# Rounds of two token tiles in the stage between two attention loops

## The chip, the cores and the metric

The kernel runs on one core of one Trainium2 chip. The metric is the device time of one execution in microseconds (us). A core has a matrix engine (PE, whose weight loads the profile shows apart as PEld), three engines for elementwise work (VectorE: DVE; ScalarE: ACT; GpSimd: POOL) and a queue that issues transfers (SyncE: SP). Each engine works through its own instructions in a fixed order and waits on semaphores. Matrix products land in PSUM, in banks; everything else is in SBUF or in HBM.

## The reference

Four residual blocks on 2048 tokens of width 576: grouped attention with one key and value head (A), linear attention with learned feature maps (B), A again, B again, with the same weights in both rounds.

```python
def _A_ref(x, wq, wk, wv, wo):          # 32 query heads of 18, one key and one value head
    q = heads(x @ wq); k = x @ wk; v = x @ wv
    p = _softmax(einsum("bhqd,bkd->bhqk", q, k) * Dh ** -0.5)
    return merge(einsum("bhqk,bkd->bhqd", p, v)) @ wo

def _B_ref(x, wqkv, w_phi, wo):
    q, k, v = split_heads(x @ wqkv)
    pq = einsum("bhsd,hdf->bhsf", q, w_phi); pk = einsum("bhsd,hdf->bhsf", k, w_phi)
    phi_q = concat([_softmax(pq), _softmax(-pq)]); phi_k = concat([_softmax(pk), _softmax(-pk)])
    kv = einsum("bhsf,bhsd->bhfd", phi_k, v); z = einsum("bhsf->bhf", phi_k)
    return merge(einsum("bhqf,bhfd->bhqd", phi_q, kv) / (einsum("bhqf,bhf->bhq", phi_q, z) + 1e-6)) @ wo

x = x + _A_ref(_layernorm(x), A_wq, A_wk, A_wv, A_wo)
x = x + _B_ref(_layernorm(x), B_wqkv, B_w_phi, B_wo)
x = x + _A_ref(_layernorm(x), A_wq, A_wk, A_wv, A_wo)
x = x + _B_ref(_layernorm(x), B_wqkv, B_w_phi, B_wo)
```

## The kernel before

The 2048 tokens are 16 token tiles of 128 (tile 0 to tile 15), and two tiles are a pair. The program has an opening, two long attention loops (`attend`, with its scores at L598, exponentials at L1131 and weighted sums at L906), a stage between the loops, and a closing stage. While a loop runs the attention of block A, it also does the key side of block B for most tiles and stores the query features of each tile (`pht`, 540 KB a tile) in HBM.

The stage between the loops is about this. For each tile, `token_tile` loads the stored features (L721 and L722, called by `load_features`) and the tile's residual `xt` (L1703) and then goes through these steps, with a `yield STAGE` as the border of a step:

- **read-out** (`read_out`, L829): 22 products of features and the state `kvb` into two PSUM banks (44 matmul records in the profile), then on DVE the division by the denominators (L836 to L839) into `xo`;
- **transposes of `xo`** (`transposed`, L310 four times and L314 once), whose result is split into a high and a low part: ACT copies the high part (L133, L316), DVE forms the low part (L136, L319), into `xs`;
- **projection** (`project`, L259): 28 products with `wob`, two banks, added to the residual on DVE (L324), which is stored (L1711);
- **norm** of the new residual: statistics on DVE (L285 to L289), the reciprocal root on POOL (L291, L293), the scaling on ACT (L300, L301) into `xn`;
- **transposes of `xn`** (L310, L314), split in the same way into one half of `xsc`, which holds a pair.

When a pair has its `xsc`, `project_queries` makes the **query projection** of the pair for the next loop: five blocks of 14 products (L467), each copied out by ACT (L492) and DVE (L499 for the low part, L501 for the squares), then stored (L503, and L509 for the keys). After that come **the norms** of the queries: two transposes (L519) and five small products (L523), read by DVE (L520, L524 to L529). The first scores of the next loop (L598) are issued among the last pairs by `early`.

All products of this stage take their PSUM bank from seven in turn (`Banks`), so a block of products must wait until the bank that was given out seven blocks earlier has been read. The stored features have two buffers (`room`: even tiles in one, odd tiles in the other), so the load for tile n + 2 waits until tile n has been read out. `xn` has one buffer.

What sets the order is a scheduler that takes the instructions in the order in which the code writes them, as far as each engine's waits allow. In the stage the code writes them as `pipelined` steps its jobs: one new tile joins in each round, and each active tile, oldest first, is carried one step. So consecutive rows on PE belong to different tiles at different steps. `settle` runs that generator with the jobs of the tiles, the waiting query projections (`late`, which also holds three leftover feature jobs, `flips`) and `early`.

Of the kernel before, what the change touches and what calls it, by code (L numbers as in the profile page):

```python
# [9 lines left out]
F32 = mybir.dt.float32  # L10
# [52 lines left out]
def kernel(ctx, tc, x_in, wq, wk, wv, wo, wqkv, w_phi, wob, out):  # L63
# [232 lines left out]
    def layer_norm(i, stats, pool, E, tag="xn"):  # L296
        rstd, bias = stats[i]
        xn = pool.tile([P, 5 * P], F32, name=tag)
        if E is A:
            A.activation(xn[:, :D], xres[i], AF.Identity, scale=rstd, bias=bias)  # L300
            A.activation(xn[:, D:], xn[:, 512:D], AF.Copy)  # L301
        else:
            V.tensor_scalar(xn[:, :D], xres[i], rstd, bias, op0=ALU.mult, op1=ALU.add)
            V.tensor_copy(xn[:, D:], xn[:, 512:D])
        return xn
# [149 lines left out]
    def project_queries(p, layer, w, xsc, bw, pool, ps, norms):  # L455
# [25 lines left out]
        for m in (*range(KT - 1), KT - 1) if opening else (KT - 1, *range(KT - 1)):  # L481
# [22 lines left out]
            if m == KT - 1:  # L504
                queue = nc.gpsimd if p == NT // PAIR - 1 else nc.sync
                for j, piece in enumerate(KPIECES):
                    for base in (0, ROWT):
                        row = base + j * DH
                        queue.dma_start(kst[row : row + DH, keys].bitcast(F32),  # L509
                                          pc[KROW : KROW + DH, piece, :].bitcast(F32))  # L510
        if opening:
            st["third"]()
        elif layer == 0 and p <= 2:
            st["pinned"].extend(traced(nc)[written_from:])
# [333 lines left out]
    def next_queries(i, stats, layer, st, xpool, sp, ps):  # L848
        p, tt = divmod(i, PAIR)
        xn = layer_norm(i, stats or ln_stats([i]), xpool, A)  # L850
# [8 lines left out]

    def paired(jobs, beside):  # L860
        def advance_each(*tiles):
            for job in tiles:
                for v in job:
                    if v is STAGE:
                        break

# [68 lines left out]
    THIRD = 3  # L935
    WE = V
# [415 lines left out]
    def settle(layer, ps, jobs):  # L1352
        st.update(ready=0, head=[], roomed="", begun=0)
        run(pipelined(jobs, st["late"], early(layer, st, ps)))
        st["slot"] = (ps.turn - 1) % 7 // 2 + 1

    with first, ExitStack() as ps:
# [58 lines left out]
        settle(0, ps, [setup(), *pair, *following, *third, *[first_tile(i) for i in range(3 * PAIR, 4 * PAIR)],  # L1416
# [29 lines left out]
    for layer in range(LAYERS):  # L1446
# [200 lines left out]
        with psx, tc.tile_pool(name=f"s{layer + 1}", bufs=2) as sp, tc.tile_pool(name=f"s{layer + 1}q", bufs=1) as spq:  # L1647
# [50 lines left out]
            def token_tile(i):  # L1698
# [6 lines left out]
                if not last:  # L1705
                    yield STAGE
# [3 lines left out]
                else:  # L1710
                    nc.sync.dma_start(xd[i], xres[i])  # L1711
                    yield STAGE
                    yield from next_queries(i, None, layer + 1, st, bw, sp, ps)
# [9 lines left out]
            else:  # L1723
                settle(layer + 1, ps, jobs)
# [27 lines left out]
```

## Time and profile before

| | us |
|---|---|
| median of 3 runs | 2601.93 (2600.37 to 2603.1) |
| the profiled execution | 2601.51 |
| its span in the trace | 2599.7 |
| PE busy in the span | 2571.9 |
| ACT busy in the span | 2161.1 |
| DVE busy in the span | 1240.1 |

Between the profiled execution and its span lie 1.8 us that the trace doesn't show. In the trace the first loop's last sums end at 1172.6 us, the first read-out of the stage starts at 1216.2 us, and the first score of the second loop's head is at 1399.8 us. In the lists of groups a row says line, engine, operation, tile written and read, shape and count, then busy time and mean of one; in the rows in order of time the first two numbers are start and duration, and what stands in brackets is the idle time of the engine ahead of the row and what ended it.

### The profile page before, as it was taken

The page shows a single profiled execution, that of the slowest core. Times are in us where ns is not written, and L with a number is a line of the kernel's source. Part 1 is how long each engine was busy: PE and PEld are TensorE (multiplying, and loading weights), DVE is VectorE, ACT ScalarE, POOL GpSimd, SP SyncE. Part 2 cuts the span into 40 slices and gives each one's busy share as a digit, 9 for nine tenths or more (in the row PEclk, how much of TensorE's full clock was granted, in tenths as well). Part 3 has the DMA queues.
Part 4 walks back from the last instruction along what each step waited for, and adds up shares of the span by engine and source line. Part 5 has one row for each costly group of instructions (what it writes and reads, how often), then busy time and mean ns, then how long its engine had stood idle before and what let it go on. Part 6 is the DMA issues. An engine that isn't in the chain of part 4 may idle for free. (4 is left out here: it accounts for less than half of the span.)

```text
span 2599.7 us, 55726 instructions
## 1 busy us (share of the span) xinstructions
PE 2571.9 (99%) x22002; PEld 1427.6 (55%) x22002; DVE 1240.1 (48%) x2828; ACT 2161.1 (83%) x2583; POOL 89.5 (3%) x185
## 2 busy tenths in 40 slices
PE   8999999999999999999999999999999999999999
PEld 7634444444444444439996344444444444444499
DVE  7435554444444444427774324444444444444275
ACT  6799999999999999993336999999999999999821
POOL 1000000000000000002000000000000000000010
PEclk9999999999999999999999999999999999999999
DMA  6574442222222222226644212222222222222164
GB/s 207 148 176 139 129 130 61 61 56 55 57 59 58 58 57 61 61 54 186 201 132 147 79 48 61 60 56 61 57 61 62 61 61 61 61 52 58 45 206 142
DMA packets 491247, 232.97 MB, mean 90 GB/s; under 512 B 237902, under 2 KB 458166, under 8 KB 490978
## 3 DMA queue, kind: packets, MB, share of 16 engines
q1 hardware_dynamic: 490002, 227.04, 33.1%
q8 instruction: 176, 2.88, 0.5%
q0 software_dynamic: 976, 2.29, 0.3%
q14 instruction: 93, 0.76, 0.1%
HBM read 130.62 MB, written 96.67 MB: 87 GB/s over the span
## 5 line engine op out<-in xcount | busy, mean ns | idle before, releaser
L1131 ACT ACTIVATE pt<-sc 128x1024 f32<-128x1024 f32 x2032 | 1923.6, 1061 | 134.8 <-PE sc L598 114.0
L598 PE MATMUL sc<-qst,kst 56*128 56x512 f32 x3840 | 687.3, 450 | 1.5 <-ACT pt L1131 1.4
L598 PEld LDWEIGHTS sc<-qst,kst 56*128 56x128 f32 x3840 | 317.1, 184 | 555.2 <-ACT pt L1131 507.6
L906 PE MATMUL acc<-pt,vst 128*32 128x512 f32 x4096 | 510.6, 600 | 0.2 <-DVE vb L663 0.2
L906 PE MATMUL ps<-pt,vst 128*32 128x512 f32 x4048 | 481.2, 598 | 0.0
L906 PEld LDWEIGHTS ps<-pt,vst 128*32 128x32 f32 x4048 | 108.6, 109 | 224.4 <-issue 223.3
L906 PEld LDWEIGHTS acc<-pt,vst 128*32 128x32 f32 x4096 | 98.6, 108 | 200.7 <-issue 189.5
L324 DVE TENSOR_TENSOR xc<-xc,acc 128x288 f32<-128x288 f32 x59 | 26.8, 454 | 330.5 <-PE acc L259 330.5
L632 DVE COPY featq<-ps 128x288 f32<-128x288 f32 x52 | 23.8, 458 | 267.4 <-PE ps L259 267.4
L259 PE MATMUL ps<-wahi,xs 128*128 128x288 f32 x684 | 145.6, 300 | 0.0
L259 PE MATMUL ps<-wchi,xs 128*128 128x288 f32 x576 | 127.4, 306 | 0.0
L259 PE MATMUL acc<-wdhi,on 128*128 128x288 f32 x531 | 117.5, 306 | 0.0
L259 PEld LDWEIGHTS ps<-wahi,xs 128*128 128x128 f32 x684 | 111.9, 188 | 2.1 <-issue 1.7
L259 PE MATMUL ps<-walo,xs 128*128 128x288 f32 x380 | 111.1, 296 | 0.0
L467 PE MATMUL ps<-xsc,wbhi 128*128 128x256 f32 x576 | 108.5, 286 | 0.7 <-ACT xsc L133 0.6
L291 POOL TENSOR_TENSOR rstd<-var,neghalf 128x1 f32<-128x1 f32 (+1 forms) x57 | 33.2, 583 | 2156.3 <-DVE mv L289 2139.4
L259 PE MATMUL acc<-wahi,xs 128*128 128x288 f32 x468 | 103.8, 307 | 2.4 <-DVE turned L1039 1.3
L259 PEld LDWEIGHTS ps<-wchi,xs 128*128 128x128 f32 x576 | 94.1, 188 | 16.2 <-issue 15.8
L133 ACT ACTIVATE xs<-ps 128x512 fp32r<-128x512 f32 x36 | 21.5, 596 | 95.8 <-PE ps L310 95.8
L259 PEld LDWEIGHTS acc<-wdhi,on 128*128 128x128 f32 x531 | 86.5, 187 | 21.2 <-issue 21.2
L632 DVE COPY featk<-acc 128x288 f32<-128x288 f32 x52 | 23.8, 457 | 153.1 <-PE acc L259 153.1
L259 PE MATMUL ps<-wclo,xs 128*128 128x288 f32 x320 | 94.3, 295 | 0.0
(266 smaller groups left out, 3150.0 us busy)
## 6 DMA issues: line engine op xcount, KB each, us to landing
qst<-qd SPq DMA_DIRECT2D x360, 72.0 KB
od<-parts SPq DMA_DIRECT2D x512, 36.0 KB
pht<-phi SPq DMA_DIRECT2D x32, 540.0 KB
qd<-pc SPq DMA_DIRECT2D x64, 256.0 KB
on<-od SPq DMA_DIRECT2D x60, 256.0 KB
phi<-pht SPq DMA_DIRECT2D x104, 144.0 KB
xd<-xc SPq DMA_DIRECT2D x33, 288.0 KB
flipped<-pht SPq DMA_DIRECT2D x112, 72.0 KB
```

What stands on the lines that cost most here:

```text
L133: A.activation(dst_hi, src, AF.Copy)
L259: T.matmul(dst, xs[:, slot, :], w[half][:, k, c0 : c0 + HALF], start=(n == 0), stop=(n == last))
L291: G.tensor_tensor(rstd, var, neghalf[:, :n], op=ALU.pow)
L324: V.tensor_add(xr, xr, po)
L467: T.matmul(po, lhs, xsc[:, slot, :], start=(n == 0), stop=(n == LASTP))
L598: T.matmul(sc, kst[head_rows(h), t * P : (t + 1) * P], q[head_rows(h), h // 2, :], start=True, stop=True)
L632: V.tensor_copy(e[:, hs, 0, :], src)
L906: T.matmul(acc[32 * j : 32 * j + 32, :], vst[:, t, :], pts[j], start=first, stop=last)
L1131: A.activation(pt, sc, AF.Exp, scale=SCALE)
```

## The change

The generator that runs the stage is replaced. `settle` takes it as an argument: the opening keeps `pipelined`, the stage between the loops gets `middle`. `middle` works in rounds on pairs: a step of both tiles of a pair is written together. In the code of a round stand, in this order, the transposes of `xo` of one pair and of `xn` of the pair before, the norms of the queries, two read-outs, two projections, and one pair's query projection. The jobs in `beside` (the feature jobs, and `early` as `fill`) get their step at fixed places of a round. Further edits: `token_tile` loses one empty step; `xn` of odd tiles gets a buffer of its own (`sp` beside `bw`); and the query projection of the last pair but one is cut after its second block by a step of its own (`HALFWAY`), into which the last pair's transposes go.

```diff
-    def layer_norm(i, stats, pool, E, tag="xn"):
+    def layer_norm(i, stats, pool, E, tag="xn", bufs=None):
         rstd, bias = stats[i]
-        xn = pool.tile([P, 5 * P], F32, name=tag)
+        xn = pool.tile([P, 5 * P], F32, name=tag, bufs=bufs)
...
+            if layer and p == NT // PAIR - 2 and m == HALFWAY:
+                yield STAGE
...
-        xn = layer_norm(i, stats or ln_stats([i]), xpool, A)
+        xn = layer_norm(i, stats or ln_stats([i]), xpool, A, bufs=1 if layer else None)
...
+    def middle(jobs, beside, fill):
+        pairs = [jobs[i : i + PAIR] for i in range(0, NT, PAIR)]
+        asked = [*beside]
+        del beside[:]
+
+        def step():
+            advance_each(*asked)
+            next(fill, None)
+
+        advance_each(*pairs[0])
+        step()
+        query = None
+        for n in range(len(pairs) + 1):
+            closing = n == len(pairs) - 1
+            if n < len(pairs):
+                advance_each(*pairs[n])
+            if 0 < n < len(pairs):
+                advance_each(*pairs[n - 1])
+            if query is not None:
+                run(query)
+            step()
+            yield STAGE
+            if n + 1 < len(pairs):
+                advance_each(*pairs[n + 1])
+            if n + 2 < len(pairs):
+                advance_each(*pairs[n + 2])
+            if n < len(pairs):
+                advance_each(*pairs[n])
+                advance_each(*pairs[n])
+            step()
+            yield STAGE
+            if n:
+                for job in asked if n == 1 else ():
+                    run(job)
+                for job in pairs[n - 1]:
+                    run(job)
+                query = beside.pop()
+                advance_each(query)
+            if closing:
+                advance_each(*pairs[n])
+                advance_each(query)
+        run(query)
+        for _ in fill:
+            pass
...
-    def settle(layer, ps, jobs):
+    def settle(layer, ps, order, jobs):
         st.update(ready=0, head=[], roomed="", begun=0)
-        run(pipelined(jobs, st["late"], early(layer, st, ps)))
+        run(order(jobs, st["late"], early(layer, st, ps)))
...
-                if not last:
-                    yield STAGE
                 yield from read_out(i, pht, st, sp, ps)
...
-                    yield from next_queries(i, None, layer + 1, st, bw, sp, ps)
+                    yield from next_queries(i, None, layer + 1, st, sp if i % PAIR else bw, sp, ps)
...
-                settle(layer + 1, ps, jobs)
+                settle(layer + 1, ps, middle, jobs)
```

No engine gets an instruction more or less: the same instructions stand in another order on PE, DVE, ACT and SP between the first read-out of the stage and its end, and POOL's order is the same. In the changed file the lines behind the insert in `project_queries` are two higher: L831 is the read-out (L829 before), L521 and L525 the norms (L519 and L523).

**First place, PE in the opening of the stage.** Before, with buffer numbers: `pht_14641` is tile 2, the last rows of whose read-out stand first, `pht_14693` is tile 3.

```order
L829 MATMUL ps_14749<-kvb_14442,pht_14641 64x57
L829 MATMUL ps_14770<-kvb_14442,pht_14641 64x57 x4
L829 MATMUL ps_14770<-kvb_14442,pht_14641 64x38 x2
L699 MATMUL ps_14798<-idf_85,featq_14244 108x128 x4
L699 MATMUL ps_14804<-idf_85,featq_14244 108x128 x4
L699 MATMUL ps_14810<-idf_85,featq_14244 108x128 x2
L699 MATMUL ps_14810<-idf_85,featq_14244 72x128
L310 MATMUL ps_14817<-idf_85,xn_14712 128x128 x4
L314 MATMUL ps_14824<-idf_85,xn_14712 128x128
L310 MATMUL ps_14844<-idf_85,xo_14748 128x128 x4
L314 MATMUL ps_14851<-idf_85,xo_14748 128x128
L829 MATMUL ps_14856<-kvb_14442,pht_14693 64x57 x16
```

In the changed kernel, at the same place: the first row is the end of tile 2's read-out, `pht_14658` is tile 3, `pht_14663` is tile 4.

```order
L831 MATMUL ps_14793<-kvb_14442,pht_14653 64x38 x2
L831 MATMUL ps_14806<-kvb_14442,pht_14658 64x57 x16
L831 MATMUL ps_14827<-kvb_14442,pht_14658 64x57 x4
L831 MATMUL ps_14827<-kvb_14442,pht_14658 64x38 x2
L310 MATMUL ps_14840<-idf_85,xn_14751 128x128 x4
L314 MATMUL ps_14847<-idf_85,xn_14751 128x128
L310 MATMUL ps_14851<-idf_85,xn_14766 128x128 x4
L314 MATMUL ps_14858<-idf_85,xn_14766 128x128
L831 MATMUL ps_14865<-kvb_14442,pht_14663 64x57 x16
L831 MATMUL ps_14886<-kvb_14442,pht_14663 64x57 x4
L831 MATMUL ps_14886<-kvb_14442,pht_14663 64x38 x2
L310 MATMUL ps_14943<-idf_85,xo_14771 128x128 x4
```

Before, 28 projections stood between the read-outs of tiles 3 and 4 (and pieces of tile 2's read-out among projections); now tile 4's read-out follows tile 2's with only tile 3's read-out and ten transposes between. Nine more transposes follow, then tile 5's read-out.

**Second place, PE in a round.** Before, one tile's transposes, its neighbour's read-out, then the norms of the queries:

```order
L310 MATMUL ps<-idf,xo 128x128 x4
L314 MATMUL ps<-idf,xo 128x128
L829 MATMUL ps<-kvb,pht 64x57 x20
L829 MATMUL ps<-kvb,pht 64x38 x2
L519 MATMUL ps<-idf,featk 128x128 x2
```

In the changed kernel, directly behind a pair's query projection (L467):

```order
L310 MATMUL ps<-idf,xo 128x128 x4
L314 MATMUL ps<-idf,xo 128x128
L310 MATMUL ps<-idf,xo 128x128 x4
L314 MATMUL ps<-idf,xo 128x128
L310 MATMUL ps<-idf,xn 128x128 x4
L314 MATMUL ps<-idf,xn 128x128
L310 MATMUL ps<-idf,xn 128x128 x4
L314 MATMUL ps<-idf,xn 128x128
L521 MATMUL ps<-idf,featk 128x128 x2
```

Behind these stand the five products of the norms, two read-outs in a row, 56 projections in a row and the 70 products of the next query projection. Before, a read-out, five transposes and 28 projections lay between the end of a query projection and its norms; now 20 transposes do.

**Third place, ACT ahead of the first query projection.** Before, from the copies of the pair's second half of `xsc` (the first two rows) to the first copies out of the query projection (the last two):

```order
L133 ACTIVATE xsc<-ps 128x4x128
L316 ACTIVATE xsc<-ps 128x128
L133 ACTIVATE xs_14938<-ps 128x512
L316 ACTIVATE xs_14938<-ps 128x128
L704 ACTIVATE phs<-ps 108x512 x2
L704 ACTIVATE phs<-ps 108x256
L704 ACTIVATE phs<-ps 72x128
L300 ACTIVATE xn<-xt,lnb_15030,rstd_15028 128x576
L301 ACTIVATE xn<-xn 128x64
L133 ACTIVATE xs_15068<-ps 128x512
L316 ACTIVATE xs_15068<-ps 128x128
L492 ACTIVATE pc<-ps 128x256
```

In the changed kernel, ahead of the second query projection (tiles 2 and 3), whose products stand on PE directly behind the ten transposes of `xn`:

```order
L133 ACTIVATE xsc<-ps 128x4x128
L300 ACTIVATE xn<-xt,lnb_15425,rstd_15423 128x576
L316 ACTIVATE xsc<-ps 128x128
L301 ACTIVATE xn<-xn 128x64
L133 ACTIVATE xsc<-ps 128x4x128
L300 ACTIVATE xn<-xt,lnb_15440,rstd_15438 128x576
L316 ACTIVATE xsc<-ps 128x128
L301 ACTIVATE xn<-xn 128x64
L492 ACTIVATE pc<-ps 128x256
```

Both halves of `xsc` are now copied one after the other, with a norm of another tile (L300) between them, and nothing on PE stands between the transposes and the products that read `xsc`.

More of the change, by code (lines that the diff above doesn't have):

```diff
@@ L858, in next_queries, with advance_each @@
             st["late"].append(project_queries(p, layer, st["wq"], xsc, bw, st["pieces"], ps, st["norms"]))
-    def paired(jobs, beside):
[L861 to L865, printed above, removed]
+    def advance_each(*tiles):
+        for job in tiles:
+            for v in job:
+                if v is STAGE:
+                    break
+    def middle(jobs, beside, fill):
[40 more added lines that the diff above has]
+            pass
+    def paired(jobs, beside):
         pairs = [jobs[i : i + PAIR] for i in range(0, NT, PAIR)]
@@ L935 @@
     THIRD = 3
+    HALFWAY = 1
     WE = V
@@ L1415 @@
         opened = len(traced(nc))
-        settle(0, ps, [setup(), *pair, *following, *third, *[first_tile(i) for i in range(3 * PAIR, 4 * PAIR)],
+        settle(0, ps, pipelined, [setup(), *pair, *following, *third, *[first_tile(i) for i in range(3 * PAIR, 4 * PAIR)],
                        pause(), *[first_tile(i) for i in range(4 * PAIR, NT)]])
```

## The prediction

> **What bounds the kernel now.** I read the page's busy times, then busy time and clock by stretches of the stage that changes, then PE's rows in order of time there, and last the waits. The page and the stretches:
>
> ```profile
> PE 2571.9 (99%) x22002; PEld 1427.6 (55%) x22002; DVE 1240.1 (48%) x2828; ACT 2161.1 (83%) x2583; POOL 89.5 (3%) x185
> ...
> 1220.00:1250.00 30.00, 29.51 (x379) 27.80 (x379) 24.29 (x79) 12.09 (x29) 6.77 (x10) 1.00 0.86 243
> 1250.00:1300.00 50.00, 50.00 (x567) 48.82 (x564) 37.40 (x121) 16.75 (x41) 3.86 (x10) 1.00 0.63 188
> 1300.00:1350.00 50.00, 50.00 (x547) 48.60 (x544) 37.58 (x123) 15.84 (x41) 3.89 (x10) 1.00 0.45 139
> ```
>
> In a stretch's row stand its length, busy time of PE, PEld, DVE, ACT and POOL, the granted clock, the DMA share and GB/s. The stage is PE's: busy 50.00 of 50.00 us from 1250 on, and 29.51 of 30 before, at full clock. DVE is next with three quarters. So a new order can gain only in two ways: PE's own instructions get cheaper where equal kinds stand together, or the half microsecond of idle time goes. It can lose as much as it makes PE wait, and PE has no wait to trade in. The DMA share is 0.86 in the opening of the stage and halves later.
>
> **What a change of kind costs PE.** PE's rows in order of time, one round and the opening (number one the start, number two the duration; PE overlaps its rows, so I use differences of starts):
>
> ```profile
> 1227.02 0.76 PE L829 MATMUL ps<-kvb,pht 108*64 108x57 f32 x18 [0.49 <-DMA pht<-phi]
> 1227.71 0.40 PE L259 MATMUL ps<-wahi,xs 128*128 128x288 f32 x1
> ...
> 1228.45 0.56 PE L829 MATMUL ps<-kvb,pht 108*64 108x57 f32 x12
> 1228.94 0.54 PE L259 MATMUL ps<-wahi,xs 128*128 128x288 f32 x2
> ...
> 1232.34 0.66 PE L829 MATMUL ps<-kvb,pht 108*64 108x57 f32 x14
> 1232.93 1.41 PE L699 MATMUL ps<-idf,featq 128*108 128x128 f32 x11
> ...
> 1331.46 0.60 PE L310 MATMUL ps<-idf,xn 128*128 128x128 f32 x4
> 1331.90 0.27 PE L314 MATMUL ps<-idf,xn 128*128 128x128 f32 x1
> 1331.93 0.38 PE L259 MATMUL ps<-wahi,xs 128*128 128x288 f32 x1
> 1332.14 0.30 PE L259 MATMUL ps<-walo,xs 128*128 128x288 f32 x1
> ...
> 1335.75 0.60 PE L310 MATMUL ps<-idf,xo 128*128 128x128 f32 x4
> 1336.39 1.48 PE L829 MATMUL ps<-kvb,pht 108*64 108x57 f32 x44
> 1337.80 0.44 PE L519 MATMUL ps<-idf,featk 128*128 128x128 f32 x2
> ```
>
> A read-out in one piece takes 1337.80 - 1336.39 = 1.41 us. Tile 2's, in three pieces, takes 0.69 + 0.49 + 0.59 = 1.77, so a further cut costs 0.18. A projection's first product takes 0.21 (1331.93 to 1332.14) where (1335.75 - 1331.93) / 28 is 0.14 for one on average, so a further projection block costs about 0.08. Four transposes take 0.44, or 0.11 each; ten in a row are 1.10, and the same ten as five ahead of a projection (0.47) and five ahead of a read-out (0.64) are 1.11: joining transposes gains nothing.
>
> From the order of both kernels I counted blocks of one kind on PE between the first read-out and the second loop's first score: read-outs 19 before and 9 after, projections 19 and 11, transposes 32 and 15, 103 and 68 in all. Term **one: 10 x 0.18 + 8 x 0.08 = 2.4 us gained**. It is between 1.4 (a joined pair of whole read-outs saves perhaps 0.10, not 0.18) and 2.9 (the missing transposes pay too). Term **two: tile 2's wait of 0.49 for its features goes: 0.5 gained**, since tile 2 is now read later, with its load issued at the same place; at worst it stays.
>
> **The opening: features come too late.** Two buffers hold features, so tile 4's load can start when tile 2 is read out. In the changed order, tile 4's read-out follows tile 2's behind one read-out (1.41) and ten transposes (1.10): 2.5 us of PE work. What a load takes: SP's rows in order of time, and rows of the DMA issues.
>
> ```profile
> 1218.25 1.16 SPq L721 DMA_DIRECT2D pht<-phi  x1
> ...
> 1227.56 0.48 SPq L222 DMA_DIRECT2D wblo<-wqd  x1
> 1232.65 0.32 SPq L1703 DMA_DIRECT2D xt<-xd  x1
> 1233.07 0.35 SPq L721 DMA_DIRECT2D pht<-phi  x1
> ...
> pht<-phi SPq DMA_DIRECT2D x15, 540.0 KB
> ...
> kst<-pc POOLq DMA_DIRECT2D x6, 18.0 KB, 2.3
> ```
>
> Tile 2's load was issued at 1218.25 and PE was released at 1227.02: 8.8 us, with weights and other features in the same queue. The other end: an 18 KB transfer lands 2.3 us after its issue, and 540 KB at the stretch's 243 GB/s are 2.2 us: 4.5 us, an estimate. Tile 4's load now comes when the next loop's weights are nearly all in (their last issue is at 1227.56), so it lies nearer the low end: I take 6. Ahead of it, SP has one residual load (L1703), which waits for a norm on ACT to free its buffer: before, the issue came 0.7 us behind the start of the last piece (1232.34 to 1233.07); I take 0.8. Term **three: 0.8 + 6 - 2.5 = 4.3 us of waiting**, between 0.5 + 4.5 - 2.5 = 2.5 and 1.3 + 8.8 - 2.5 = 7.6. The ten transposes also wait for two norms on ACT, but that wait lies within these. Tile 5's load lands a transfer (2.2) behind tile 4's, and PE has 1.41 + 9 x 0.11 = 2.4 us of work between: 0.3, from 0 to 2. What is queued behind the waiting read-out on PE are the 56 projections of tiles 2 and 3, and nothing else can fill PE. Later rounds issue loads a whole round (22 us) ahead: no wait there.
>
> **The pieces on ACT and DVE.** Groups by form from 1258 to 1380 us; the last number before the second bar is the mean of one in ns:
>
> ```profile
> L499 DVE TENSOR_TENSOR pc<-ps,pc 128x256 fp32r<-128x256 f32 x27 | 11.4, 423 | 18.2 <-ACT pc L492 18.2
> L501 DVE TENSOR_TENSOR featk<-pc 128x256 bf16<-128x256 f32 x27 | 11.3, 418 | 0.4 <-ACT pc L492 0.2
> L136 DVE TENSOR_TENSOR xs<-ps,xs 128x512 fp32r<-128x512 f32 x11 | 7.3, 663 | 1.1 <-ACT xs L133 1.0
> L838 DVE TENSOR_TENSOR xo<-ps,den 128x432 f32<-128x432 f32 x10 | 6.1, 606 | 0.0
> L319 DVE TENSOR_TENSOR xs<-ps,xs 64x128 fp32r<-64x128 f32 x11 | 3.2, 295 | 0.3
> ...
> L492 ACT ACTIVATE pc<-ps 128x256 fp32r<-128x256 f32 x26 | 10.0, 384 | 34.4 <-PE ps L467 33.1 <-DMA kst<-pc 1.3
> L300 ACT ACTIVATE xn<-xt,lnb,rstd 128x576 f32<-128x576 f32 x10 | 8.7, 868 | 15.2 <-POOL lnb L293 15.2
> L133 ACT ACTIVATE xsc<-ps 128x512 fp32r<-128x512 f32 x12 | 7.2, 600 | 10.4 <-PE ps L310 10.2
> ...
> L316 ACT ACTIVATE xsc<-ps 128x128 fp32r<-128x128 f32 x12 | 3.3, 277 | 0.0
> L301 ACT ACTIVATE xn<-xn 128x64 f32<-128x64 f32 x12 | 3.1, 256 | 0.3
> ```
>
> *Second query projection.* Its products read both halves of `xsc` and stand directly behind ten transposes. ACT's order there is copy, norm, copy, tail, copy: 0.60 + 0.87 + 0.28 + 0.26 + 0.60 = 2.6 us after the first four transposes (0.44, and some 0.2 until they show on ACT); PE is through after 1.1. Rows overlap by about 0.1 each, so 2.2 + 0.64 - 1.1. Term **four: 1.7 us**. Nothing, if ACT is let through earlier; 2.6, if the norm itself comes late. Before, projections lay between and hid it.
>
> *Each full round.* The norms of the queries need, in DVE's order, the last block's L499 and L501 and the low parts of the pair's `xo`, whose banks the norms' products reuse (a bank comes back after seven blocks: the ninth and tenth of the round take those of the second and third). DVE: 0.42 + 0.42 + 0.66 + 0.30 + 0.66 + 0.30, less 0.08 of overlap each, is 2.3, behind ACT's 0.38 and 0.2 of delay: 2.9. PE has 20 x 0.11 + 0.27 = 2.5. So 0.4 is missing, and small waits ahead of it add up: I take 0.55. There are five such rounds. Term **five: 2.8 us**, from 0 (before, DVE kept up in every round) to 5 (all four low parts must be through, 1.0 a round).
>
> *First transposes.* Tiles 0 and 1 are read out in a row; DVE's division takes some 1.9 a tile (0.61 of it the row L838), so the second tile's `xo` is late for PE, which has a few projections of leftover work: term **six: 0.5**, 0 to 1.9.
>
> At the end, the cut query projection puts 42 of its products (5.0 us at 0.12) between the last projections and the transposes of their norms, and 28 (3.4) behind them; the norm's path (residual, statistics, root, scaling) sums to some 3.3 and the copies to 2.2, so both stay hidden; uncovered they would cost up to 3.
>
> **Sum.** -2.4 - 0.5 + 4.3 + 0.3 + 1.7 + 2.8 + 0.5 = +6.7 us. Against the profiled execution's 2601.51 (span 2599.7 and 1.8 around it) that is 2608.2. The median of the runs shown lies 0.42 above that execution, so I predict **2608.6 us**.
>
> **Rivals.** *The joined blocks win: not slower.* The mechanism is term one on an engine that is always busy; it decides if tile 4's features land within 2.5 us of tile 2's last read-out and the splits keep pace, so that no new wait outgrows 2.9 us. Then 2601.5 - 2.9 = 2598.6, within the bound of no change. For it: PE is 50.00 of 50.00. Against it: 540 KB alone need 2.2 us, and two other transfers' time comes on top. Chance 0.21.
>
> *DVE sets the round.* DVE is busy 37.58 of 50; with its work bunched, each of five rounds could lose 1.5 rather than 0.55: 2608.6 + 4.8 = 2613.4. For it, 20 transposes leave four low parts at once; against it, the queries' products (8.4 us) leave DVE room. Chance 0.12.
>
> *The clock falls in the wait.* PE's rows at the start of the program, the first wait in brackets:
>
> ```profile
> 8.12 1.12 PE L310 MATMUL ps<-idf,xn 128*128 128x128 f32 x4 [8.12 <-ACT xn L300]
> ...
> 13.04 1.91 PE L467 MATMUL ps<-xsc,wbhi 128*128 128x256 f32 x8
> 14.75 1.05 PE L467 MATMUL ps<-xsc,wblo 128*128 128x256 f32 x4
> ...
> 17.51 1.11 PE L467 MATMUL ps<-xsc,wbhi 128*128 128x256 f32 x8
> 18.46 0.64 PE L467 MATMUL ps<-xsc,wblo 128*128 128x256 f32 x4
> ```
>
> After 8 us of idling, eight products take 14.75 - 13.04 = 1.71 us; at 17.51 eight of the same take 0.95. So PE starts at about half speed after a long wait and needs until about 16 us to leave it. If the opening's wait does the same, some 5.5 us run at half speed and 2.8 are lost on top: 2611.4. Against it: the wait is 4.3, not 8, and in two pieces with transposes between. Chance 0.10. [...]
>
> *The order changes nothing*, because waits make it the same in time: 2602; the moved rows speak against it. Chance 0.02.
>
> **Chances.** Forecast 0.55, the others 0.21, 0.12, 0.10 and 0.02. A measurement of this kernel can tell about 0.2%, or 5.2 us. The forecast's low end (terms three to five near their low bounds, 0.09) and most of the first rival (0.18) and the last are within it: same 0.29. The rest of the first rival: faster 0.03. Slower 0.68. The range: all low bounds together give 2601, all high ones over 2619; leaving out a tenth on either side, and reaching to the first rival's upper half, 2600 to 2617.
>
> **What would show it.** Step one: a projection block of 56 takes about 7.5 us and two read-outs 2.7. Step three: one PE wait of over 2.5 us ahead of tile 4's read-out, put down to the load of `pht`. Step four: one of 1 to 2.6 us ahead of the second L467 block, by ACT. Step five: 0.3 to 1.0 a round ahead of L521 or L525, by DVE. The prediction is wrong if tile 4's features wait for nobody, or if the waits at the ends of rounds stay below 0.2.

## The result, and the profile after

| | before | after |
|---|---|---|
| median, us | 2602.51 (6 runs, 2600.37 to 2603.99) | 2612.4 (6 runs, 2611.08 to 2614.12) |
| the profiled execution, us | 2601.51 | 2611.08 |
| its span, us | 2599.7 | 2609.1 |
| first read-out of the stage, us | 1216.2 | 1215.3 |
| first score of the next loop's head, us | 1399.8 | 1408.8 |

The ratio is 1.0040, with a 95% interval of 1.0029 to 1.0051: slower by 9.9 us, and more than the 0.2% that a measurement can tell. From the first read-out to the first score the stage takes 193.5 us where it took 183.6, which is 9.9 more. The spans differ by 9.4, since the changed kernel enters the stage 0.9 sooner and takes 0.4 longer behind it. The two rows of the changed kernel are:

```profile
1215.28 2.76 PE L831 MATMUL ps<-kvb,pht 108*64 108x57 f32 x88
...
1408.80 0.50 PE L600 MATMUL sc<-wclo,kst 56*128 56x512 f32 x1
```

In the changed file the loads of features are L723 and L724, the residual's load L1751 and its store L1757, and the 22 transposes of leftover features L701. First the stretches of the stage, in the columns of before:

```profile
PE 2574.6 (99%) x22002; PEld 1428.8 (55%) x22002; DVE 1239.7 (48%) x2828; ACT 2159.5 (83%) x2583; POOL 89.3 (3%) x185
...
1220.00:1250.00 30.00, 25.37 (x305) 24.27 (x304) 22.09 (x73) 6.76 (x15) 6.04 (x8) 0.89 0.71 209
1250.00:1300.00 50.00, 48.13 (x521) 46.91 (x520) 32.66 (x106) 17.68 (x45) 3.67 (x10) 1.00 0.63 188
1300.00:1350.00 50.00, 49.40 (x527) 47.74 (x526) 34.63 (x115) 15.83 (x43) 3.68 (x10) 1.00 0.49 146
```

The whole program's shares have hardly moved, and they hide the loss. The stretches show it: PE lacks 4.6 of 30 us in the opening (0.5 before), 1.9 of the next 50 and 0.6 of the third stretch, where it lacked nothing. The clock's column says 0.89 in the opening. The waits of PE in the stage, as total, times and longest:

```profile
PE ps L831 <- DMA pht<-phi: 4.0, 1, 4.0
PE ps L467 <- ACT xsc L133: 1.6, 1, 1.6
PE ps L525 <- DVE xs L136: 1.4, 5, 0.3
PE ps L310 <- ACT xn L300: 0.7, 1, 0.7
```

They come to 7.7 us. The opening again in PE's rows in order of time, ahead of them SP's rows of the loads:

```profile
1226.24 0.32 SPq L1757 DMA_DIRECT2D xd<-xt  x1
...
1231.53 0.32 SPq L1751 DMA_DIRECT2D xt<-xd  x1
1231.95 0.35 SPq L723 DMA_DIRECT2D pht<-phi  x1
```

```profile
1228.92 2.76 PE L831 MATMUL ps<-kvb,pht 108*64 108x57 f32 x88
1231.62 0.66 PE L310 MATMUL ps<-idf,xn 128*128 128x128 f32 x4
...
1233.04 0.66 PE L310 MATMUL ps<-idf,xn 128*128 128x128 f32 x4 [0.66 <-ACT xn L300]
1233.53 0.27 PE L314 MATMUL ps<-idf,xn 128*128 128x128 f32 x1
1237.78 2.58 PE L831 MATMUL ps<-kvb,pht 108*64 108x57 f32 x44 [3.97 <-DMA pht<-phi]
1240.28 1.12 PE L310 MATMUL ps<-idf,xo 128*128 128x128 f32 x4
...
1242.39 2.17 PE L831 MATMUL ps<-kvb,pht 108*64 108x57 f32 x44
...
1244.58 0.38 PE L259 MATMUL ps<-wahi,xs 128*128 128x288 f32 x1
```

Tiles 2 and 3 are read in 2.70 us (1228.92 to 1231.62). Then come the ten transposes, and PE stands still for 3.97 us until tile 4's features are there, 5.8 us after their issue. Behind the wait tile 4's read-out takes 2.50 us (1237.78 to 1240.28) and tile 5's 2.11, where one took 1.35 just before, and no wait is shown in either. Single microseconds of the same kernel say why; the third number from the end is the granted clock:

```profile
1236.00:1237.00 1.00, 0.00 (x0) 0.00 (x0) 0.00 (x0) 0.00 (x0) 0.00 (x0) 1.00 0.76 210
1237.00:1238.00 1.00, 0.23 (x4) 0.26 (x6) 0.00 (x0) 0.00 (x0) 0.00 (x0) 0.56 1.01 284
1238.00:1239.00 1.00, 1.00 (x23) 1.00 (x23) 0.00 (x0) 0.00 (x0) 0.00 (x0) 0.50 0.88 246
...
1243.00:1244.00 1.00, 1.00 (x24) 1.00 (x24) 0.17 (x2) 0.10 (x1) 0.00 (x0) 0.52 0.86 260
1244.00:1245.00 1.00, 1.00 (x24) 0.95 (x21) 0.66 (x3) 0.14 (x1) 0.00 (x0) 1.00 0.19 55
```

The clock falls to 0.5 at 1237.12 (0.56 is 0.12 of a microsecond at full clock and 0.88 at half) and comes back at 1243.96, after 6.8 us. From 1237.78 on PE counts as busy all the time. One full round, in PE's rows:

```profile
1331.56 0.60 PE L310 MATMUL ps<-idf,xo 128*128 128x128 f32 x4
...
1332.65 0.60 PE L310 MATMUL ps<-idf,xn 128*128 128x128 f32 x4
...
1333.91 0.44 PE L521 MATMUL ps<-idf,featk 128*128 128x128 f32 x2
1334.63 0.71 PE L525 MATMUL ps<-featk,sel 128*128 128x256 bf16 x5 [0.28 <-DVE xs L136]
1335.27 2.76 PE L831 MATMUL ps<-kvb,pht 108*64 108x57 f32 x88
1337.96 0.40 PE L259 MATMUL ps<-wahi,xs 128*128 128x288 f32 x1
```

The list of waits gives the norms 0.28 us a round. The starts give more: the two transposes take 0.72 (1333.91 to 1334.63), and the sums 0.64.

### The profile page after: what moved, and what is told of

The parts are those of the page before. It is cut to its first block, busy times and chain, and to the rows that moved or that the text cites. A ratio compares the mean times of both kernels' runs of the same rounds, so it can differ in the third digit from the quotient of the medians.

```text
span 2609.1 us, 55697 instructions
## 1 busy us (share of the span) xinstructions
PE 2574.6 (99%) x22002; PEld 1428.8 (55%) x22002; DVE 1239.7 (48%) x2828; ACT 2159.5 (83%) x2583; POOL 89.3 (3%) x185
## 5 line engine op out<-in xcount | busy, mean ns | idle before, releaser
L467 PE MATMUL ps<-xsc,wbhi 128*128 128x256 f32 x576 | 108.2, 285 | 0.7 <-ACT xsc L133 0.7
L467 PEld LDWEIGHTS ps<-xsc,wbhi 128*128 128x128 f32 x576 | 90.9, 192 | 1.7 <-ACT xsc L133 1.1
```

Source lines behind the costliest of these rows:

```text
L467: T.matmul(po, lhs, xsc[:, slot, :], start=(n == 0), stop=(n == LASTP))
```

## The experiments

All twelve kernels are edits of the changed one; each ratio is to the kernel before, with its 95% interval. The runs have 5 to 11 timings each, and an interval is 5 to 7 us wide: under 2 or 3 us a time alone decides nothing. Then rows are read, and the length of the stage in the profile, from the start of the first read-out to the start of the first score: 183.65 us before and 193.52 in the changed kernel. There is one profile of each kernel.

**Cover the load.** One move in `middle`: in the second round tiles 2 and 3 are projected ahead of tile 4's read-out.

```diff
+            if n == 1:
+                advance_each(*pairs[n])
+                advance_each(*pairs[n])
             if n + 1 < len(pairs):
                 advance_each(*pairs[n + 1])
...
-            if n < len(pairs):
+            if n < len(pairs) and n != 1:
                 advance_each(*pairs[n])
                 advance_each(*pairs[n])
```

> In the second round, tiles 2 and 3 have their output projections ahead of tile 4's read-out instead of behind it: the 56 products that take 7.6 us in the changed kernel stand where TensorE waited 4.0 us for tile 4's features, and nothing else is moved. Theory (the wait for the features, and the half clock that it brings on, are two thirds of the 9.4 us): the wait shrinks from 4.0 to under 1 us, no row shows a granted clock under 1.0 between 1228 and 1250 us, the two read-outs take 2.7 instead of 4.6 us, and the time falls by about 6 us, to 2605.5 to 2607.5. Rival (the features come late because the room, or an engine that works on tiles 2 and 3, comes late as well, so that the load is pushed back with the read-out): a wait of 2 to 4 us stays ahead of tile 4's read-out and the time falls by less than 2 us.

Measured: 2605.73 us, 1.0014 (1.0005 to 1.0023), 6.7 below the changed kernel. The theory held. The stretches of this run:

```profile
1230.00:1240.00 10.00, 9.09 (x131) 7.81 (x130) 8.54 (x30) 4.87 (x12) 3.10 (x6) 1.00 0.78 244
1240.00:1250.00 10.00, 10.00 (x148) 9.79 (x147) 7.13 (x28) 3.92 (x9) 1.46 (x4) 1.00 0.54 158
```

PE is busy 19.1 of 20 us, the clock never falls, and the load's wait is gone. The stage takes 187.68 us, 5.8 less than in the changed kernel, and the wait was 3.97 of them. Some two thirds of the loss hung on that one place.

**Work that nobody needs, in place of the wait.** Products into a spare bank ahead of tile 4's read-out, first 24 and then 52:

```diff
+            if n == 1:
+                filler = bank(psa, "acc", [P, HALF])
+                for j in range(FILL):
+                    T.matmul(filler, st["wob"][0][:, 0, :P], st["wob"][0][:, 0, :HALF], start=True, stop=True)
             if n + 1 < len(pairs):
...
+    FILL = 24
```

> 24 products of 128x288 into a bank of PSUM that nobody reads are added to the reference's computation ahead of tile 4's read-out, where TensorE waits 4.0 us; the output stays as it is. 21 of them stand in the wait itself (21 x 0.136 us = 2.9 us, all within the wait), 3 are issued earlier and cost 0.4 us. The features come no sooner, so that the wait and the products together still end when the load lands. Theory (the half clock of 6.8 us behind the wait is brought on by the pause itself): the granted clock stays at 1.0, the two read-outs take 2.7 instead of 4.6 us and the ten transposes about 1.0 instead of 2.1, so that more work gives less time: 2.9 - 0.4 = 2.5 us less, 2609 to 2611. Rival (the read-outs are slow because their features come piecemeal, or the clock falls whatever TensorE does there): the blocks keep 4.6 and 2.1 us, and the time rises by 0.4 to 1 us.

Measured: 2617.41 us, 1.0061 (1.0047 to 1.0075): 5 us more, not 2.5 less. The step that failed was that the features come when they came before. PE's rows and the clock of this run:

```profile
1235.27 3.01 PE L893 MATMUL acc<-wahi 128*128 128x288 f32 x21
1241.95 1.64 PE L831 MATMUL ps<-kvb,pht 108*64 108x57 f32 x44 [3.67 <-DMA pht<-phi]
1244.82 2.57 PE L831 MATMUL ps<-kvb,pht 108*64 108x57 f32 x44 [1.23 <-DMA pht<-phi]
```

```profile
1235.00:1240.00 5.00, 3.28 (x26) 3.05 (x24) 2.18 (x6) 1.29 (x4) 0.00 (x0) 1.00 0.80 197
1240.00:1245.00 5.00, 1.82 (x48) 1.74 (x50) 0.82 (x4) 0.00 (x0) 0.00 (x0) 0.81 0.60 167
1245.00:1250.00 5.00, 5.00 (x56) 4.58 (x54) 1.68 (x7) 1.23 (x3) 0.00 (x0) 0.51 0.57 165
```

The features came 8.4 us behind the end of the read-outs of tiles 2 and 3 (1233.55), not 6.2 as in the changed kernel. So a pause of 3.67 us was left, tile 5 waited too, and there was a half clock behind it. The run decides nothing between the pause and other causes, hence the longer one, with FILL at 52.

> As the run with 24 products added ahead of tile 4's read-out, but with 52: 49 of them (some 6.9 us) stand between the transposes of tiles 0 and 1 and that read-out, where the shorter run still left a pause of 3.67 us that ended with a half clock of 6.8 us. The products are added to the reference's computation and nobody reads them. Theory (a pause of TensorE, and not the transfers or the kind of work, brings the half clock on): no pause of over 1 us is left, the granted clock is 1.0 throughout, the two read-outs take 2.7 us and the ten transposes behind them 1.1 to 1.5, and with 28 more products the time is 4 to 5 us below that of the shorter run, 2612 to 2614 us, level with the changed kernel that has none. Rival (the clock falls there whatever TensorE does): a half clock stands behind the products all the same, and the time is 2617 us or more.

Measured: 2618.78 us, 1.0066 (1.0053 to 1.0080). By the clock the theory held, by the time it didn't. PE's rows, and the stretches:

```profile
1233.96 6.70 PE L893 MATMUL acc<-wahi 128*128 128x288 f32 x49
1240.59 1.48 PE L831 MATMUL ps<-kvb,pht 108*64 108x57 f32 x44
1243.03 1.48 PE L831 MATMUL ps<-kvb,pht 108*64 108x57 f32 x44 [0.96 <-DMA pht<-phi]
1244.44 0.66 PE L310 MATMUL ps<-idf,xo 128*128 128x128 f32 x4
...
1254.64 1.36 PE L701 MATMUL ps<-idf,featq 128*108 128x128 f32 x11
...
1422.46 0.73 PE L600 MATMUL sc<-wclo,kst 56*128 56x512 f32 x2 [3.71 <-issue]
```

```profile
1230.00:1240.00 10.00, 9.57 (x136) 9.29 (x133) 5.79 (x24) 3.56 (x8) 2.33 (x5) 1.00 0.62 193
1240.00:1250.00 10.00, 8.41 (x126) 7.29 (x125) 5.66 (x20) 1.43 (x4) 0.00 (x0) 1.00 0.65 190
```

With the pause filled, the clock stays at 1.0 in the opening and a read-out takes 1.41 us. In all six kernels here without the pause ahead of tile 4's read-out the clock stays at 1.0 there, and in all seven with it (3.67 to 5.50 us) it falls to a half: in the opening the half clock came with the pause. The time is some 5 us above the range, and the profile shows where. The stage takes 195.4 us, 1.9 more than in the changed kernel, where the theory had it level. Tile 5 waits 0.96 us. The transposes and projections behind the read-outs take 10.2 us (1244.44 to 1254.64) where the changed kernel needs 9.74 (2.19 and 7.55): at full clock PE arrives sooner and waits for DVE's division, in two listed waits of 0.27 and 0.2. And where the next loop is entered PE stands for 3.71 us that the profile puts down to no event ("issue"), while the kernel before and the changed one wait 0.8 and 0.7 us there. Behind that gap the clock falls to a half again, from 1422.98 to 1426.40. The gap was not tried by itself.

**Issue the load sooner.** SP's order only: tile 6's residual load, which waited for a store, goes behind the loads of tiles 4 and 5 by a manual dependency.

```diff
                 load_features(pht, spills[layer], i)
+                if not last and i == 2 * PAIR + 1:
+                    st["behind"] = traced(nc)[-1].name
                 if i not in left:
                     xres[i] = sp.tile([P, D], F32, name="xt", bufs=6)
                     nc.sync.dma_start(xres[i], xd[i])
+                    if not last and i // PAIR == 3:
+                        tc.add_manual_dep(traced(nc)[-1], st["behind"], NOSYNC, reason="order")
```

> Only SP's order is changed, and there two rows: the residual load of tile 6 stands behind the feature loads of tiles 4 and 5 instead of ahead of them, and tile 1's store stands ahead of them. In the changed kernel that residual load waited 3.9 us on SP for a store to land, from 1227.5 to 1231.5 us, and the feature load of tile 4 was issued behind it at 1231.95, though its room was free when tile 2's read-out ended at about 1230.3. Theory (1.5 us of the wait of 4.0 are a queue's order and not the transfer): tile 4's load is issued 1.2 to 1.6 us sooner against the end of tile 2's read-out, TensorE waits 2.4 to 2.8 us for it, and the time falls by 1.5 us if the granted clock still goes to a half behind the wait, by 4.4 us if it stays at 1.0 behind the shorter one. Rival (the transfers of the opening share the queue's bandwidth, so the load lands when the stores and weights ahead of it are through, whenever it is issued): the wait stays at 3.5 to 4.5 us and the time within 1 us.

Measured: 2611.68 us, 1.0036 (1.0022 to 1.0050), against 1.0040 for the changed kernel. The rival held. SP's rows of this run (L1761 is the store):

```profile
1230.17 0.32 SPq L1761 DMA_DIRECT2D xd<-xt  x1
1231.01 0.33 SPq L723 DMA_DIRECT2D pht<-phi  x1
...
1237.13 0.64 SPq L1753 DMA_DIRECT2D xt<-xd  x1
```

The read-outs ended at 1232.18 here, so the issue came 1.5 us sooner against them. Yet PE was released at 1238.84, 7.8 us after it and not 5.8, and waited 4.48 us. From 1230 to 1235 us the DMA share is 0.96 at 347 GB/s here, and 0.61 at 188 in the changed kernel. That more transfers side by side slow the load fits this, but was not tried by itself. In the changed kernel, the two of the next experiment, this one, the split blocks and the kernel without the cut the wait was 4.0, 4.7, 5.5, 4.5, 3.9 and 5.1 us, all with the same opening on PE: one profile's 3.97 is at the low end of what the load costs. Against the end of the read-outs PE was released after 6.7 us here and after 6.1 to 7.5 in the other five. So no gain is seen, but one profile beside such a spread can't rule out a part of the 1.5 us.

**Cover the query projection, move the norms.** The second move puts the transposes of tiles 2 and 3 for their queries ahead of the third round's projections, the third puts the norms behind the read-outs:

```diff
+            if n == 2:
+                for job in pairs[1]:
+                    run(job)
             if n < len(pairs):
                 advance_each(*pairs[n])
```

> In the third round the transposes of tiles 2 and 3 for their queries are put ahead of the 56 output projections of tiles 4 and 5 instead of behind them, so that ScalarE has 7.6 us to copy them before the second query projection reads them. Theory (term four was a real cost): the wait of 1.58 us before the second block of the query projection is gone, nothing takes its place, and the time falls by 1.6 us, to 2610 to 2611.5. Rival (the normalized tiles are not there so early, so that the transposes wait for VectorE or ScalarE instead): a wait of 1 us or more stands before the ten transposes, and the time falls by less than 0.7 us.

```diff
-            if query is not None:
-                run(query)
             step()
             yield STAGE
             if n + 1 < len(pairs):
                 advance_each(*pairs[n + 1])
+            if query is not None:
+                run(query)
```

> In each round the two sums of squares for a pair's query norms are put behind the next pair's two read-outs (2.7 us) instead of ahead of them. Theory (term five was a real cost, 0.65 us of waiting for VectorE in each of five rounds): the ten waits before the sums shrink to under 0.1 us each, no other wait takes their place, and the time falls by about 3 us, to 2608.5 to 2610. Rival (VectorE sets the round, since its share of a round goes on and what it does later comes later): the waits come back before the read-outs, the transposes or the scores of the next loop, 0.4 us or more a round, and the time falls by less than 1 us.

Measured: 2611.14 us, 1.0035 (1.0021 to 1.0049), and 2610.95 us, 1.0035 (1.0022 to 1.0049). Each took its wait away in its profile, and smaller ones came up: 0.3 us for DVE's division with the second move, and 0.53 for the low parts ahead of one read-out and 0.2 ahead of the next loop's scores with the third. The load's wait was 4.7 and 5.5 us in them, so neither time settles it. A round of the second of these kernels:

```profile
1290.09 2.76 PE L831 MATMUL ps<-kvb,pht 108*64 108x57 f32 x88
1292.79 0.44 PE L521 MATMUL ps<-idf,featk 128*128 128x128 f32 x2
1293.06 0.71 PE L525 MATMUL ps<-featk,sel 128*128 128x256 bf16 x5
1293.53 0.38 PE L259 MATMUL ps<-wahi,xs 128*128 128x288 f32 x1
```

The norms take 0.27 + 0.47 = 0.74 us where they took 1.36: 0.62 a round, more than twice the 0.28 that the list of waits had. Therefore combinations with the first move, which leaves no wait to take a gain up:

> The three moves at once: tiles 2 and 3 projected ahead of tile 4's read-out, their transposes for the queries ahead of the projections of the third round, and the norms of the queries behind the two read-outs. Alone they were measured at 6.7, 1.3 and 1.5 us below the changed kernel, the last two beside a wait for tile 4's features that had grown by 0.7 and 1.5 us. Theory (the three waits are separate costs, and without the long wait the second and third move are worth 1.6 and 3.0 us): 2612.4 - 6.7 - 1.6 - 3.0 = 2601.1 us, between 2600 and 2602.5, level with the kernel before or a little faster. Rival (ScalarE and VectorE give out what they give out, and the waits move on together): 2603 to 2605.5 us, with a wait of over 1 us that none of the three runs alone had.

> The first two moves without the third: tiles 2 and 3 projected ahead of tile 4's read-out, and their transposes for the queries ahead of the projections of the third round; the norms of the queries stay ahead of the read-outs. The first move alone was measured at 2605.7 us, all three at 2602.1, so that 3.6 us belong to the second and third together. Theory (each is worth the wait that it takes away): the wait of 1.58 us before the second query projection goes and the five waits of the rounds stay, 2604.1 us, between 2603.5 and 2604.8. Rival (the transposes put forward only move ScalarE's work, and the third move brought all): the time stays at 2605.2 us or more.

> The first and the third move without the second: tiles 2 and 3 projected ahead of tile 4's read-out, and the norms of the queries behind the two read-outs; the transposes of tiles 2 and 3 for the queries stay directly ahead of the second query projection. All three moves were measured at 1.0001 of the kernel before (2602.1 us), the first and second at 1.0015 (2606.1 us), the first alone at 1.0014 (2605.7 us). Theory (the second move is worth the wait that it takes away, and its own measurement was off): the wait of 1.58 us is back and the ratio is 1.0005 to 1.0008, 2603.3 to 2604.4 us. Rival (what the second move takes away on TensorE comes back elsewhere, and the third brought all): 1.0000 to 1.0003, 2602 to 2603 us.

| moves | us | ratio (95% interval) | stage in the profile, us |
|---|---|---|---|
| 1 | 2605.73 | 1.0014 (1.0005 to 1.0023) | 187.68 |
| 1, 2 | 2606.13 | 1.0015 (1.0006 to 1.0024) | 186.38 |
| 1, 3 | 2604.11 | 1.0009 (1.0000 to 1.0018) | 185.28 |
| 1, 2, 3 | 2602.12 | 1.0001 (0.9992 to 1.0010) | 184.06 |

The three together held the theory: 2602.12 lies in its range of 2600 to 2602.5. By the medians the second move on the first alone brought nothing, which was its rival's case, and on the first and third 2.0 us, which was the theory's; but the intervals overlap. The lengths of the stage agree better: the second move takes 1.30 us off with the first and 1.22 with the first and third, the third move 2.40 and 2.32. For the second this is its wait of 1.58 less the 0.35 and 0.28 us of waiting for DVE's division that stand there instead; for the third it is five times 0.62 less the 0.53 and 0.2 that came up. The median of the first two moves doesn't show this gain. In their profile the clock falls to a half behind the stage, at the entry of the next loop (1406.84 to 1410.26), though no wait there was over 0.8 us; in the profiles of the other three rows it doesn't fall (mean granted clock 1.0). Whether that takes up the gain wasn't measured.

**Split the blocks again.** In five rounds the read-outs and projections alternate as before:

```diff
+            if 1 < n < len(pairs) - 1:
+                for one, other in zip(pairs[n + 1], pairs[n]):
+                    advance_each(one, other)
-            if n + 1 < len(pairs):
+            elif n + 1 < len(pairs):
                 advance_each(*pairs[n + 1])
...
             if n < len(pairs):
                 advance_each(*pairs[n])
-                advance_each(*pairs[n])
+                if not 1 < n < len(pairs) - 1:
+                    advance_each(*pairs[n])
```

> In five rounds (tiles 4 to 13) the two read-outs and the two projections stand by turns again, read-out, projection, read-out, projection, as in the kernel before, with all else in the rounds as in the changed kernel: 10 blocks more on TensorE, no work more. Theory (term one, a change of kind costs 0.18 us for a read-out and 0.08 us for a projection): each of the five rounds has 0.2 to 0.3 us more of busy time between the start of its first read-out and the end of its last projection, and the time rises by 1.0 to 1.3 us. Rival (the order of blocks is free, and what was gained beside the waits came from the transposes or from tile 2's wait): under 0.1 us a round, and no change of time.

Measured: 2615.11 us, 1.0050 (1.0037 to 1.0064). One round of this kernel, from the first read-out to the query projection, then the same round of the changed kernel:

```profile
1313.12 1.48 PE L831 MATMUL ps<-kvb,pht 108*64 108x57 f32 x44
...
1323.70 1.82 PE L467 MATMUL ps<-xsc,w 128*128 128x256 f32 x14
```

```profile
1313.00 2.76 PE L831 MATMUL ps<-kvb,pht 108*64 108x57 f32 x88
...
1323.26 1.83 PE L467 MATMUL ps<-xsc,w 128*128 128x256 f32 x14
```

10.58 against 10.26 us: two blocks more cost 0.32 us, with no wait in either, just over the theory's 0.3. The time rose by 2.7 us, more than its 1.0 to 1.3, but the intervals overlap. The stage in this profile took 193.81 us, only 0.29 more than in the changed kernel. The wait for the load was the same (3.94), but the half clock behind it lasted 3.4 us instead of 6.8 (1238.78 to 1242.18), and from tile 4's read-out to the leftover transposes it took 13.13 us instead of 14.35. With these 1.22 put back, the ten blocks cost 1.5.

**Leave out the cut at the end.**

```diff
-            if layer and p == NT // PAIR - 2 and m == HALFWAY:
+            if layer and p == NT // PAIR - 2 and m == -1:
                 yield STAGE
```

> The query projection of the last pair but one isn't cut: its 70 products stand in one piece, and the last pair's transposes come behind them, directly ahead of the last pair's own query projection. Theory (the cut hides the last pair's copies behind 28 products, as the forecast held): a wait of 1.6 us for ScalarE's copies, as it stands ahead of the second query projection, appears ahead of the last one, and the time rises by 1.5 to 3 us. Rival (ScalarE is through with the copies anyway at that place, since no normalization of a later tile stands between them): waits of under 0.4 us in all and a change of under 0.5 us.

Measured: 2613.44 us, 1.0042 (1.0029 to 1.0056), against 1.0040 with the cut. The rival held by the list of waits: one wait of 0.17 us for DVE's low part is all that appeared. The starts give more: from the norms of the last full round to the row with three of the first scores it takes 30.24 us (1380.27 to 1410.51) where it took 29.65 (1379.91 to 1409.56) with the cut. So the cut is worth 0.6 us, and not the 1.5 to 3 of the theory.

**A fourth move.** With the first three, the leftover transposes go among those of tiles 2 and 3, and the ten of tiles 0 and 1 behind the projections:

```diff
-            if 0 < n < len(pairs):
+            if 1 < n < len(pairs):
                 advance_each(*pairs[n - 1])
...
             if n == 1:
                 advance_each(*pairs[n])
+                for job in asked:
+                    run(job)
                 advance_each(*pairs[n])
+                advance_each(*pairs[0])
...
-                for job in asked if n == 1 else ():
-                    run(job)
```

> The three moves and a fourth in the opening: the leftover feature transposes (22, some 2.4 us) stand among the transposes of tiles 2 and 3 instead of behind tile 4's read-out, and the ten transposes of tiles 0 and 1 come behind the projections of tiles 2 and 3. With three moves the opening still had ten transposes in 1.96 and ten in 1.48 us, and 56 projections in 8.48, against 1.26, 1.09 and 7.55 in a full round: 2.0 us of small waits. Theory (work that doesn't hang on them fills them): at least half of it comes back, 2600 to 2601.2 us, below the kernel before. Rival (ScalarE and VectorE must copy the leftover features out first, and what hangs on them comes later by as much): no gain, 2602 us or more.

Measured: 2601.18 us, 0.9997 (0.9988 to 1.0006). The theory's time came, at its upper end, but the interval holds the kernel before: no version of this order was shown to beat it in time. The stage took 183.03 us in the profile, 1.0 less than with three moves and 0.6 less than before. Behind it, at the entry of the next loop, the clock fell to a half here too (1403.56 to 1406.98).

## Why the prediction was right, and where it fell short

The side and the range held: 2612.4 us is slower, within 2600 to 2617. The forecast of 2608.6 was 3.8 too low, and the rival of the falling clock (2611.4, chance 0.10) came nearer. Most waits came at the places and by the causes that were named; what was missing is mostly the clock.

- **One, joined blocks (2.4 gained).** Right, a little small: the split round shows 0.32 us for two blocks, 0.16 each, and 18 blocks less at that price are 2.9, the bound that the prediction named.
- **Two, tile 2's wait (0.5 gained).** Right: no such wait is left.
- **Three, tile 4's features (4.3 + 0.3 lost).** Right in kind, a little small: 3.97 for the load and 0.66 for the norm in the list, and 5.1 by the starts (6.16 from the end of the read-outs to tile 4's, less 1.10 for ten transposes). The residual load on SP did stand ahead of it, but with the load issued sooner PE's wait was no shorter. Tile 5 had no wait of its own; at full clock, with 52 products added, it had 0.96.
- **Four, the second query projection (1.7 lost).** Right: the wait was 1.58 us, or 1.8 by the starts (1275.04 to 1277.88, less 1.09 for ten transposes). Taking it away shortened the stage by 1.2 to 1.3, since 0.3 of waiting for DVE came in its place.
- **Five, the rounds (2.8 lost).** Right in kind, too small: the norms take 1.36 us where they took 0.82 before (1337.80 to 1338.62), and the ten transposes ahead of them 1.26 where ten take 1.09. That is 0.7 a round and 3.5 in five, where 0.55 and 2.8 were taken.
- **Six, the first transposes (0.5 lost).** About 0.3: four took 0.73 us (1217.98 to 1218.71) against 0.44.
- **The end.** It is hidden, but the cut hides little: the "up to 3" without it was 0.2 of waiting in the list and 0.6 by the starts.
- **The clock.** The step that failed stands in the third rival: "Against it: the wait is 4.3, not 8, and in two pieces with transposes between". A pause of 3.97 us in one piece was enough, and the rival came true on top of the forecast, as a cost of its own and not in the place of another case. The read-outs behind the pause took 4.6 instead of 2.7 us and the ten transposes 2.2 instead of 1.1. That is 3.0 us at most. Part of it would have been waiting for DVE at full clock too: from tile 4's read-out to the leftover transposes the changed kernel takes 14.35 us, the one with 52 products 14.05, and 0.96 of these are tile 5's wait, so that 1.3 are the clock's by this comparison. So 1.3 to 3 us are the clock's, near the 2.8 that the rival had. (In the rows of the program's start, from which the rival was taken, eight products take 1.71 us and later 0.95, but the clock's column reads 1.00 in the first 20 us; they did not show the granted clock.) In or soon behind each of the seven pauses ahead of tile 4's read-out (3.67 to 5.50 us), and behind the gap of 3.71 us, the clock fell. It also fell at the entry of the next loop in three profiles without such a pause.

The terms by the starts: -2.9 - 0.5 + 5.1 + 1.8 + 3.5 + 0.3 = 7.3, with the clock's 1.3 to 3 between 8.6 and 10.3, against 9.9 in the stage. Of the other rivals, the joined blocks did not win, since the wait came. Even with four moves, which leave none of the four waits, their 2.9 us show as no gain in time over the kernel before, and as 0.6 us in the length of the stage. Small waits are left there (0.43 us for DVE's `xo`, 0.54 for the low parts ahead of a read-out); whether such waits make up all of it wasn't measured. That DVE sets the round (1.5 each) was too much.

## What to carry to other kernels

Grouping like work on a busy engine earned 0.16 us for each block saved, and lost it at the few places where the work between a producer and its reader had been the cover: count at each reader what still stands between, loads first. Don't price a pause of the matrix engine at its length alone: with each of the seven here (3.67 to 5.50 us) came 3.4 to 6.8 us at half clock. When a profile shows slow products without a wait, read the clock in stretches of a microsecond. To see what a small wait costs, take differences of starts, since the list of waits had less than half of it in the rounds (0.28 of 0.62 us); and where the times of two kernels lie within the noise, compare the length of the stage between two rows that both have.

## What the runs showed of the hardware that was not expected

- Behind the pause ahead of tile 4's read-out the half clock lasted 6.8 us in six of seven profiles (1237.12 to 1243.96 in the changed kernel, 1238.22 to 1245.04 with the earlier load, 1243.12 to 1249.94 with 24 products added), and 3.4 us in the seventh (the split blocks, 1238.78 to 1242.18, behind a pause of 3.94 us). What decides between the two lengths is open. It need not begin in the pause: with 24 products added PE was at work again from 1241.95, and the clock fell 1.2 us later.
- A long pause was not needed every time: in three profiles (the second move alone, the first two moves, the four moves) the clock fell to a half for 3.4 us at the entry of the next loop, where no wait was over 0.8 us. The kernel before, the changed one and those with the first move, the first and third, and the first three have like waits there (0.7 to 0.8 us) and no fall. The cause is open.
- An issue 1.5 us earlier brought a 540 KB load no sooner in the one profile that there is: 7.8 us to PE's release instead of 5.8.
- 52 products more in the stage went along with a gap of 3.71 us at the entry of the next loop, some 180 us later, that no event explains. The cause is open.
